# Values from normalised x, tile-wise first FFN blocks behind an interleaved LayerNorm, and doubled tail loads, in a fused LayerNorm, attention and FFN kernel

## Chip, cores and metric

The kernel runs on one core of one Trainium2 chip. Its time is the device time of one execution in microseconds (us). A profile records one execution: its span runs from the first to the last instruction. PE is TensorE, DVE VectorE, ACT ScalarE, POOL GpSimd, and SP the engine that issues most of the DMAs. ACT issues some as well.

## What is computed

One block over x of 2048 tokens by 448, in bf16. All three results are added.

```python
def _layernorm(x, axis=-1, eps=1e-5):
    m = jnp.mean(x, axis=axis, keepdims=True)
    v = jnp.var(x, axis=axis, keepdims=True)
    return (x - m) / jnp.sqrt(v + eps)

# A: attention with feature maps, H = 16 heads of Dh = 28
qkv = (x @ wqkv).reshape(B, S, 3, H, Dh)            # then q, k, v by head
pq, pk = q @ w_phi, k @ w_phi                       # per head
phi_q = concat([softmax(pq), softmax(-pq)]);  phi_k = concat([softmax(pk), softmax(-pk)])
kv = einsum("bhsf,bhsd->bhfd", phi_k, v);     z = phi_k summed over s
o  = (phi_q @ kv) / (phi_q . z + 1e-6);       A = o @ wo
# B: FFN with F = 1792
B = silu(x @ w1) @ w2

x = A_x
xn = _layernorm(x, axis=-1)
return x + _A_ref(xn, A_wqkv, A_w_phi, A_wo) + _B_ref(xn, B_w1, B_w2)
```

## The kernel before

The whole input, all weights and all intermediate values stay on the chip. The 2048 tokens are held as 16 tiles of 128 (`x_sb[:, t]`). Two tiles make a pair `p`, 0 to 7; pairs 0 to 3 are chunk 0, pairs 4 to 7 chunk 1. The 448 columns of x don't divide by 128: they are three blocks of 128 and a tail of 64. Two tiles of a pair share the tail block: the transposed input `xnT` has seven blocks, 0 to 2 (`JA`) for one tile, 4 to 6 (`JB`) for the other, and block 3 (`JT`) with the tail of one tile in partitions 0 to 63 and that of the other in 64 to 127. So the last 64 rows of a weight are needed in both halves of the partitions. Most matmuls run on 64 rows, two at a time in the two halves (`halves`): that is a pair of matmuls. A unit of 7 pairs is given to PE as two halves, `way` 0 (three pairs and the tail pair) and `way` 1 (three pairs).

Stages, in order of time:

1. Start-up, to about 19 us: load x and weights, LayerNorm statistics on DVE (`ln_stats`, L625 and L627), the power -1/2 on POOL (`ln_rstd`, L638), the norm on DVE (`ln_norm`, L647), transposes on PE, their eviction on ACT or DVE (L694, L668), and the first FFN blocks: f-blocks 0 to 7 on pair 0 alone (`ffn1_full`, 128-row matmuls of 128 columns), then 8 to 13 on pairs 0 and 1 (`ffn1_unit` with two f-blocks and 256 columns).
2. To about 33 us the rest of the first FFN layer of chunk 0, and `fold`: products of the projection weights and w_phi, from weights that DVE has transposed (`wq_tr`).
3. To about 66 us keys, values and queries, with exp on ACT (`k_macro`, `v_macro`, `q_group`), the sums `phi_k` on DVE and POOL.
4. The first FFN layer of chunk 1 beside the attention on DVE, and then the second FFN layer, the output projection and the stores.

The order on PE is written out by hand: operations are put in the list `W`, and `weave` makes each of them follow the one before. DVE's order is written out by `chain`. What is left free is ordered by a list scheduler with estimated durations. An engine executes its instructions in that order, so one that waits holds up those behind it. A DMA waits on its own queue only for what it depends on; the loads of the second half of x (`load_x1`, four of them) and of the q and k weights (`load_wqk`) each wait until an earlier load in the list `quarters` has landed (`few`).

In the kernel before, the values of pairs 0 and 1 are made early from x that isn't normalised: `tr_full(p, True, ...)` transposes raw x, `v_raw` multiplies it by the value weights (`Wkv` columns 448 to 896, loaded as `wv`), `col_sums` makes the column sums of these weights, `v_keep` evicts the raw values (ACT), and later `v_scale` (POOL, L724) and `v_fix` (DVE, L731) correct them with the mean and the power, which four small DMAs (`rm_move`, L1078) bring into the order of tokens. The last 64 rows of w1 are loaded into partitions 0 to 63 (two DMAs on the ACT queue) and copied to 64 to 127 by DVE (columns 0 to 511, L1058) and ACT (the other 1280). The last 64 rows of the value weights are loaded twice, once by SP and once by ACT. The loads of the start-up, in program order:

```python
load_x0(0)
load_k(Wkv, D, A_wqkv, 2 * D, 3 * D, "wv", "act")
load_x0(1)
load_tails(Wkv, D, A_wqkv, 2 * D, 3 * D, "wv")
for c0, c1 in ((0, 512), (512, 1024), (1024, 1280), (1280, FF)):
    quarters.append(load_k(w1_sb, c0, B_w1, c0, c1, "w1"))
```

Of the kernel before, what the change touches and what calls it, by code (L numbers as in the profile page):

```python
# [6 lines left out]
BF16 = mybir.dt.bfloat16  # L7
# [346 lines left out]
def bass_parallel_sum__linear_kernel_hedgehog__dense_activation_silu__prompt_kernel(  # L354
# [18 lines left out]
    with es:  # L373
# [37 lines left out]
        halfs = sb("halfs", [128, 128], BF16)  # L411
        hT1 = hT[:, 1].rearrange("p f r i q t -> p (f r i q t)")
        Ek = [Ek4[:, b] for b in range(4)] + [hT1[:, 4096 + 1920 * b:4096 + 1920 * b + EKS] for b in range(4)]
        spare = hT[:, 1].rearrange("p f r i q t -> p (f r i q t)")[:, 2 * FT * 128:]
        xrT = spare[:, 0:2 * 7 * 128].rearrange("p (b j t) -> p b j t", b=2, j=7)
        csum = spare[:, 1792:1792 + 2 * D].bitcast(F32)
        Vraw = spare[:, 2688:2688 + 8 * D].bitcast(F32).rearrange("p (b r c) -> p b r c", b=2, r=2)
# [8 lines left out]
        rm = sb("rm", [128, 2, NT], F32)  # L426
        rmP = sb("rmP", [128, 2, 4], F32)
# [82 lines left out]
        P.op("pool", d_pool(128, 0.5), lambda e: e.memset(halfs[:], 0.5), writes=[halfs[:]], name="halfs")  # L510
# [9 lines left out]
        NWARM = 6  # L520

        def warm(us=220.0):
            w, x = (nc.const_aps.tensor(1.0, [128, n], BF16) for n in (128, 512))
            o = P.op("pe", us, lambda e: e.matmul(banks[7][:], w, x, start=True, stop=True, skip_group_check=True),
                     writes=[banks[7][:]], name="warm")
            o.mode = "full"
            o.pieces = [(us, 2)]
            return o

        for i in range(NWARM):  # L530
            warm(426.0)
# [12 lines left out]
        def load_x0(q):  # L544
            if q > 0:
                load(xt_sb[:, 0, q], xa[0][:, q], 256 * D * 2, f"x0{q}")
                return
            for r, eng in ((0, "sp"), (1, "act")):
                d = slice(D * r, D * r + D)
                load(xt_sb[:, 0, q, d], xa[0][:, q, d], 128 * D * 2, "x00", eng)  # L550
# [8 lines left out]
        def load_tails(dst, d0, src, c0, c1, name):  # L559
            w = c1 - c0  # L560
            return [load(dst[64 * h:64 * h + 64, 3, d0:d0 + w], src[384:448, c0:c1], 64 * w * 2, f"{name}t{h}", ("sp", "act")[h])
                    for h in range(2)]
# [27 lines left out]
        load_x0(0)  # L590
        load_k(Wkv, D, A_wqkv, 2 * D, 3 * D, "wv", "act")
        load_x0(1)
        load_tails(Wkv, D, A_wqkv, 2 * D, 3 * D, "wv")
        for c0, c1 in ((0, 512), (512, 1024), (1024, 1280), (1280, FF)):
            quarters.append(load_k(w1_sb, c0, B_w1, c0, c1, "w1"))
            if c0 == 0:
                for b0, b1 in ((0, 512), (512, FF)):
                    load(w1_sb[0:64, 3, b0:b1], B_w1[384:448, b0:b1], 128 * (b1 - b0), "w1t", "act")
            if c0 in (0, 1024):
                load_x0(2 + c0 // 1024)  # L600
# [33 lines left out]
        def ln_rstd(t0, t1):  # L634
            v2, mm2, r2, nh = ve[:, t0:t1], mv[:, t0:t1, 1], rm[:, 0, at(t0):at(t1 - 1) + 1], neghalf[:, t0:t1]
            o = P.op("dve", 180, lambda e: e.tensor_scalar(v2, mm2, EPS_LN, None, ALU.add),  # L636
                 reads=[mm2], writes=[v2], name="ve")
            P.op("pool", 580, lambda e: e.tensor_tensor(r2, v2, nh, ALU.pow), reads=[v2, nh], writes=[r2], name="rstd")  # L638
            return o

        def ln_norm(p, t, eng="dve"):
            sl, m, r = p % NXN, mv[:, t, 0:1], rm[:, 0, at(t):at(t) + 1]
# [31 lines left out]
        def tr_full(p, raw, bs, engs=("act", "act")):  # L674

            t0, t1 = ln_tiles(p)
            dst = [banks[bs + (j > 2)][:, 128 * (j - 3 * (j > 2)):128 * (j - 3 * (j > 2)) + 128] for j in range(7)]
            if raw:
                xs = [x_sb[:, t, 128 * j:128 * j + 128] for t in (t0, t1) for j in range(3)]
                xs[3:3] = [None]  # L680
            else:
                xs = [xn_sb[:, p % NXN, 128 * j:128 * j + 128] for j in range(7)]
            ops = []
            for a, b in ((0, 3), (3, 7)):
                parts = [(dst[j], xs[j], perm4[:], True, True) for j in range(a, b) if xs[j] is not None]
                ops.append(pe(parts, [62.0] * len(parts), "x_tr" if raw else "xnT_tr", "full"))
            if raw:
                ops.append(pe([(dst[3][64 * r:64 * r + 64], x_sb[:, (t0, t1)[r], 384:448], perm4[:], True, True) for r in range(2)],
                              [62.0], "x_tr", "c64"))
            for (r, j0, j1), eng in zip(((0, 0, 3), (1, 3, 7)), engs):  # L690
                src = banks[bs + r][:, 0:128 * (j1 - j0)].rearrange("p (j t) -> p j t", t=128)
                d = xrT[:, p, j0:j1] if raw else xnT[:, j0:j1, 0, 128 * p:128 * p + 128]
                if eng == "dve":
                    chain([P.op("dve", d_dve(_cols(src)), lambda e, d=d, src=src: e.tensor_copy(d, src), reads=[src], writes=[d],  # L694
                                name="xnT_ev")])
                else:
                    act(d, src, ACTF.Identity, "x_ev" if raw else "xnT_ev")
            return ops

        def v_raw(p):  # L700

            b0 = 2 * p
            main = []
            for r in range(2):
                for k in range(3):
                    main.append((banks[b0 + r][:, 0:D], xrT[:, p, 4 * r + k], Wkv[:, k, D:2 * D], k == 0, False))
            return [pe(main[3 * r:3 * r + 3], [slot(D)] * 3, "v", "full") for r in range(2)], \
                lambda: pe(halves((banks[b0][:, 0:D], xrT[:, p, JT], Wkv[:, 3, D:2 * D]),
                                  (banks[b0 + 1][:, 0:D], xrT[:, p, JT], Wkv[:, 3, D:2 * D]), 0, False, True), [slot(D)], "v")

        def v_keep(p):
            src = psum[:, 1024 * p:1024 * p + 1024].rearrange("p (r c) -> p r c", r=2)[:, :, 0:D]
            act(Vraw[:, p], src, ACTF.Identity, "v_ev")

        def col_sums(ks):

            return pe([(banks[7][:, 0:D], halfs[:] if k == 3 else ones_bf[:], Wkv[:, k, D:2 * D], k == 0, k == 3) for k in ks],
                      [slot(D)] * len(ks), "csum", "full")

        def v_scale(p, after):  # L720

            for r in range(2):
                raw, m = Vraw[:, p, r], rmP[:, 0, 2 * p + r:2 * p + r + 1]
                P.op("pool", 1400, lambda e, raw=raw, m=m: e.tensor_scalar(raw, raw, m, None, ALU.mult),  # L724
                     reads=[raw, m], writes=[raw], name="v_scale").odeps.add(after.id)

        def v_fix(p, after):
            for r in range(2):
                dst, m = vaug[:, p, r, :, 0:DH], rmP[:, 1, 2 * p + r:2 * p + r + 1]
                r3, c3 = (a.rearrange("p (h d) -> p h d", h=H) for a in (Vraw[:, p, r], csum))  # L730
                P.op("dve", d_dve(D), lambda e, dst=dst, r3=r3, c3=c3, m=m: e.scalar_tensor_tensor(  # L731
                    dst, c3, m, r3, ALU.mult, ALU.add), reads=[Vraw[:, p, r], csum, m], writes=[dst], name="v_fix").odeps.add(after.id)
# [67 lines left out]
        def ffn1_unit(c, f0, nf=1, q0=0, nq=4):  # L800
# [8 lines left out]
            for way in range(2):  # L809
                parts = []  # L810
                for i in range(nf):
                    ws = slice((f0 + i) * 128, (f0 + i) * 128 + 128)
                    da, db = (banks[b0 + r][:, n * i:n * i + n] for r in range(2))
                    for k in range(3):
                        parts += halves((da, w1_sb[:, k, ws], xa[JA + k]), (db, w1_sb[:, k, ws], xa[JB + k]),
                                        way, way == 0 and k == 0 and i == 0, way == 1 and k == 2)
                    if way == 0:
                        w = w1_sb[:, 3, ws]
                        parts += halves((da, w, xa[JT]), (db, w, xa[JT]), 0, False, False)
# [13 lines left out]
        def ffn1_full(f0, bs, tails_first):  # L833

            main, tails = [], []
            d2 = [banks[bs + r] for r in range(2)]
            for r, j0 in ((0, JA), (1, JB)):
                for i in range(4):
                    ws, cs = slice((f0 + i) * 128, (f0 + i) * 128 + 128), slice(128 * i, 128 * i + 128)
                    main += [(d2[r][:, cs], w1_sb[:, k, ws], xnT[:, j0 + k, 0, 0:128], not tails_first and k == 0 and i == 0,  # L840
                              tails_first and k == 2) for k in range(3)]
            for i in range(4):
                ws, cs = slice((f0 + i) * 128, (f0 + i) * 128 + 128), slice(128 * i, 128 * i + 128)
                w, x = w1_sb[:, 3, ws], xnT[:, JT, 0, 0:128]
                tails += halves((d2[0][:, cs], w, x), (d2[1][:, cs], w, x), 0, tails_first and i == 0, not tails_first)

            def rows():
                return [pe(main[a:a + 12], [slot(128)] * 12, "ffn1", "full") for a in (0, 12)]

            def rest():  # L850
                return pe(tails, [slot(128)] * 4, "ffn1")
# [5 lines left out]
            return rows, rest, out  # L857
# [39 lines left out]
        def kv_unit(p, c0, name):  # L897
# [566 lines left out]
```

## Time and profile before

| what | value |
|---|---|
| runs | 151.93, 152.47, 154.23 us; median 152.47 |
| profiled execution | 151.9 us, of which the span is 150.2 |
| granted TensorE clock, mean | 1.000 |
| PE busy | 145.3 us, 97% of the span |
| DVE, ACT, POOL busy | 114.9, 86.1, 53.0 us |
| first instruction of PE | 0.82 us |
| last eviction on DVE | 147.29 to 147.91 us |

The profile's page is followed by views of the trace: windows (busy time of each engine in a stretch of the span, with the share of the 16 DMA engines and their rate), the timeline (instructions in order of time, runs of equal ones merged), the DMA issues (KB and the time from issue to landing) and the chain that ended last (followed back from the last instruction). In the names, `big` is the weight w1, `wbig` holds the weights of values, keys and queries, `xu` the normalised x, `x_sb` the input, `hT` the hidden layer and some scratch space, `EqT` scratch space too in the start-up. The matmuls of the working stages all have line L468, since one helper issues them; the first ones, on constants, are L524.

### The profile page before, as it was taken

How to read it: one execution, taken by the hardware profiler on the slowest of the kernel's cores; microseconds unless marked ns; L12 is line 12 of the kernel's file. 1: busy time of each engine (PE TensorE's matmuls, PEld its weight loads, DVE VectorE, ACT ScalarE, POOL GpSimd, SP SyncE). 2: the span in 40 equal slices, each digit the busy share in tenths (PEclk: the TensorE clock that was granted, in tenths of full speed). 3: DMA queues.
4: the chain of work that ended last, by engine and by line, in shares of the span. 5: the costliest groups of instructions: out<-in, count | busy, mean ns of one | idle time of the engine just before them, and what ended most of it. 6: DMA issues, size and time to landing. Idle time of an engine off the chain costs nothing.

```text
span 150.2 us, 5219 instructions
## 1 busy us (share of the span) xinstructions
PE 145.3 (97%) x2328; PEld 84.0 (56%) x2328; DVE 114.9 (77%) x191; ACT 86.1 (57%) x102; POOL 53.0 (35%) x55
## 2 busy tenths in 40 slices
PE   7999999999999999999999999999999999999992
PEld 2578886565545444444555545555555555448771
DVE  0898699997999998575308999999899999940072
ACT  3668868998979788999678998323322200000000
POOL 4322989979609999779300000000000000000000
PEclk9999999999999999999999999999999999999999
DMA  4998761000133543200143444450030003001013
GB/s 140 329 295 160 193 151 34 4 4 4 48 91 91 142 124 98 90 4 0 27 119 86 129 103 137 139 177 22 4 124 0 4 0 127 0 0 65 0 65 122
DMA packets 15588, 12.98 MB, mean 86 GB/s; under 512 B 5838, under 2 KB 14990, under 8 KB 15566
## 3 DMA queue, kind: packets, MB, share of 16 engines
q1 hardware_dynamic: 14782, 11.90, 28.8%
q10 hardware_dynamic: 784, 0.75, 1.6%
q8 instruction: 18, 0.29, 0.8%
q14 instruction: 4, 0.03, 0.1%
HBM read 9.89 MB, written 1.84 MB: 78 GB/s over the span
## 4 chain that ended last, share of the span: by engine, by line
PE 82%; ACT 8%; DMA 4%; issue 2%; ACTq 1%; DVE 0%
PE psum L468 82%; DMA big<-in_B_w_dram 4%; ACT hT L499 3%; ACT EqT L499 3%; ACT L499 1%; ACTq L536 1%; ACT big L499 1%; DVE big L1269 0%; ACTq L1404 0%; ACT tiny L499 0%
## 5 line engine op out<-in xcount | busy, mean ns | idle before, releaser
L468 PE MATMUL psum<-xnT,big 64*128 64x512 bf16 (+4 forms) x540 | 45.8, 313 | 0.6 <-ACT hT L499 0.6
L468 PE MATMUL psum<-w_sb,hT 64*128 64x448 bf16 (+1 forms) x504 | 44.4, 329 | 0.0
L499 ACT ACTIVATE hT<-psum 128x1024 bf16<-128x1024 f32 (+6 forms) x45 | 39.7, 918 | 7.3 <-PE psum L468 7.0
L468 PEld LDWEIGHTS psum<-xnT,big 64*128 64x128 bf16 (+1 forms) x540 | 25.4, 94 | 15.5 <-ACT hT L499 1.3
L468 PEld LDWEIGHTS psum<-w_sb,hT 64*128 64x128 bf16 x504 | 23.6, 94 | 17.3 <-issue 1.3
L499 ACT ACTIVATE big<-psum 128x896 bf16<-128x896 f32 (+1 forms) x16 | 14.8, 955 | 12.3 <-DVE scr L1218 7.2
L468 PE MATMUL psum<-wbig,xnT 64*128 64x448 bf16 x196 | 21.3, 349 | 0.0
L1269 DVE TENSOR_TENSOR big<-psum,x_sb 128x896 bf16<-128x896 f32 (+1 forms) x9 | 8.7, 986 | 12.1 <-PE psum L468 12.1
L499 ACT ACTIVATE EqT<-psum 128x1024 bf16<-128x1024 f32 x16 | 15.6, 1038 | 3.3 <-PE psum L468 3.3
L468 PEld LDWEIGHTS psum<-wbig,xnT 64*128 64x128 bf16 x196 | 9.7, 94 | 9.5 <-ACT big L499 0.3
L468 PE MATMUL psum<-xnT,wbig 64*128 64x512 bf16 x112 | 14.6, 377 | 0.1
L946 POOL TENSOR_TENSOR big<-big,Rk 128x1792 bf16<-128x1792 bf16 x4 | 12.8, 3210 | 5.0 <-DVE Rk L943 4.7
L946 POOL TENSOR_TENSOR hT<-hT,Rk 128x1792 bf16<-128x1792 bf16 (+1 forms) x5 | 12.9, 2606 | 2.1 <-DVE Rk L943 1.1
L625 DVE BATCH_NORM_STATS2 st<-x_sb 128x6 f32<-128x448 bf16 x16 | 9.8, 612 | 4.6 <-DMA x_sb<-in_A_x_dram 3.6
L499 ACT ACTIVATE xu<-psum 128x960 f32<-128x960 f32 x8 | 7.8, 976 | 7.8 <-PE psum L468 4.3
L468 PE MATMUL psum<-wbig,big 32*128 32x448 bf16 (+1 forms) x252 | 11.3, 327 | 0.0
L938 DVE TENSOR_REDUCE Sk<-hT 128x64 f32<-128x1792 bf16 (+1 forms) x5 | 8.2, 1634 | 3.1 <-ACT hT L499 3.1
L638 POOL TENSOR_TENSOR rm<-ve,neghalf 128x2 f32<-128x2 f32 (+1 forms) x9 | 6.2, 691 | 9.9 <-DVE ve L636 9.9
L647 POOL TENSOR_SCALAR xu<-x_sb,mv,rm 128x64 bf16<-128x64 bf16 (+1 forms) x8 | 9.0, 1130 | 0.7 <-POOL rm L638 0.4
L468 PEld LDWEIGHTS psum<-wbig,big 32*128 32x128 bf16 x252 | 6.9, 93 | 4.1 <-issue 1.1
L1224 DVE STREAM_TRANSPOSE big<-big 128x896 bf16<-128x896 bf16 x8 | 8.9, 1110 | 0.2
L1222 DVE TENSOR_TENSOR big<-scr 128x896 bf16<-128x896 f32 x8 | 8.7, 1093 | 0.3
(74 smaller groups left out, 140.4 us busy)
## 6 DMA issues: line engine op xcount, KB each, us to landing
x_sb<-in_A_x_dram SPq DMA_DIRECT2D x4, 448.0 KB, 3.4
x_sb<-in_A_x_dram SPq DMA_DIRECT2D x7, 224.0 KB, 5.6
wbig<-in_A_wo_dram SPq DMA_DIRECT2D x4, 392.0 KB, 3.5
out_dram<-big SPq DMA_DIRECT2D x7, 224.0 KB, 2.0
big<-in_B_w_dram SPq DMA_DIRECT2D x3, 384.0 KB, 7.1
xnT<-hT SPq DMA_DIRECT2D x16, 56.0 KB, 2.0
w_sb<-in_B_w_dram SPq DMA_DIRECT2D x2, 448.0 KB, 3.7
EqT<-in_A_wqkv_dram SPq DMA_DIRECT2D x3, 224.0 KB, 4.0
```

The lines of the kernel that those rows point to most:

```text
L468: r = e.matmul(dst, lhsT, rhs, start=start, stop=stop, skip_group_check=True)
L499: return P.op("act", d_act(_cols(src)), lambda e: e.activation(dst, src, func, scale=scale), reads=[src, *more], writes=[dst], table=table ...
L536: return P.dma(lambda e: e.dma_start(out=dst, in_=src), nbytes, writes=[dst], name=name, eng=eng)
L625: o1 = P.op("dve", 630, lambda e: e.bn_stats(st6[:, t, :], x_sb[:, t, :]), reads=[x_sb[:, t, :]], writes=[st6[:, t, :]], name="bnst")
L638: P.op("pool", 580, lambda e: e.tensor_tensor(r2, v2, nh, ALU.pow), reads=[v2, nh], writes=[r2], name="rstd")
L647: lambda e, xn=xn, xs=xs: e.tensor_scalar(xn, xs, m, r, ALU.subtract, ALU.mult),
L938: P.op("dve", d_dve(896 * n), lambda e, S3=S3, E3=E3: e.tensor_reduce(S3, E3, AXL.X, ALU.add), reads=[E3], writes=[S3], name="Sk")
L946: P.op("pool", d_pool(896 * n, 1.55), lambda e, E3=E3, R3=R3, n=n: e.tensor_tensor(E3, E3, R3[:, :, None].broadcast_to([128, 32 * n, DH]), ...
L1222: P.op("dve", d_dve(896), lambda e: e.tensor_tensor(dst, a0, a1, ALU.add), reads=[a0, a1], writes=[dst], name="oadd")
L1224: P.op("dve", d_dve(896), lambda e: e.transpose(dT, dst), reads=[dst], writes=[oT32[:, n, :, 2 * h:2 * h + 2, :]], name="oT")
L1269: P.op("dve", d_dve((c1 - c0) * ni), lambda e: e.tensor_tensor(dst, src, xs, ALU.add), reads=[src, xs], writes=[dst], name="out_ev")
```

## The change

- The path over raw x goes: `v_raw`, `v_keep`, `col_sums`, `v_scale`, `v_fix`, `scaled_mean`, the raw form of `tr_full` and the four `rm_move` DMAs. The values of pairs 0 and 1 are made by `v_macro` like those of the other pairs, evicted by ACT.
- Each tail is loaded by one DMA into all 128 partitions, from a source pattern that reads its 64 rows twice (`load_tails`). The copies of w1's tail on DVE and ACT go. The w1 tail comes in three loads (columns 0 to 511, 512 to 1023, the rest), the value weights' tail in one.
- The loads are put in another order: w1's first columns before the value weights. The first x tile pair comes in four DMAs, and five loads besides go to the ACT queue.
- The LayerNorm of the first pairs is taken tile by tile on DVE, statistics of the next tile between a tile's power and its norm.
- `ffn1_full` gives out pieces of six matmuls; they are put between the transposes of pairs 0 and 1. `ffn1_unit` and `kv_unit` can do their two halves in the other order (`ways`).
- The 6 warm-up matmuls of 512 columns become 8 of 512 and 8 of 128, and six more of 128 stand between the first transposes and the first FFN matmuls.

```diff
-        NWARM = 6
...
-        for i in range(NWARM):
-            warm(426.0)
+        for n in [512] * 8 + [128] * 8:
+            warm(n / 1.2, n)
...
+        def load_x0(q, eng="sp"):
+            load(xt_sb[:, 0, q], xa[0][:, q], 256 * D * 2, f"x0{q}", eng)
+
+        def load_x00():
+            for r in range(2):
                 d = slice(D * r, D * r + D)
-                load(xt_sb[:, 0, q, d], xa[0][:, q, d], 128 * D * 2, "x00", eng)
+                for h, eng in ((0, "sp"), (1, "act")):
+                    p = slice(64 * h, 64 * h + 64)
+                    load(xt_sb[p, 0, 0, d], xa[0][p, 0, d], 64 * D * 2, "x00", eng)
...
-        def load_tails(dst, d0, src, c0, c1, name):
-            w = c1 - c0
-            return [load(dst[64 * h:64 * h + 64, 3, d0:d0 + w], src[384:448, c0:c1], 64 * w * 2, f"{name}t{h}", ("sp", "act")[h])
-                    for h in range(2)]
+        def load_tails(dst, d0, src, c0, c1, name, eng="sp"):
+
+            a = src[384:448, c0:c1]
+            return load(dst[:, 3, d0:d0 + c1 - c0], type(a)(a.tensor, a.offset, [[0, 2], *a.ap]), 256 * (c1 - c0), name + "t", eng)
...
-        load_x0(0)
-        load_k(Wkv, D, A_wqkv, 2 * D, 3 * D, "wv", "act")
-        load_x0(1)
-        load_tails(Wkv, D, A_wqkv, 2 * D, 3 * D, "wv")
-        for c0, c1 in ((0, 512), (512, 1024), (1024, 1280), (1280, FF)):
-            quarters.append(load_k(w1_sb, c0, B_w1, c0, c1, "w1"))
-            if c0 == 0:
-                for b0, b1 in ((0, 512), (512, FF)):
-                    load(w1_sb[0:64, 3, b0:b1], B_w1[384:448, b0:b1], 128 * (b1 - b0), "w1t", "act")
-            if c0 in (0, 1024):
-                load_x0(2 + c0 // 1024)
+        load_x00()
+        quarters.append(load_k(w1_sb, 0, B_w1, 0, 512, "w1"))
+        load_x0(1, "act")
+        load_tails(w1_sb, 0, B_w1, 0, 512, "w1")
+        quarters.append(load_k(w1_sb, 512, B_w1, 512, 1024, "w1", "act"))
+        load_tails(w1_sb, 512, B_w1, 512, 1024, "w1")
+        load_x0(2, "act")
+        load_k(Wkv, D, A_wqkv, 2 * D, 3 * D, "wv")
+        load_tails(Wkv, D, A_wqkv, 2 * D, 3 * D, "wv", "act")
+        quarters.append(load_k(w1_sb, 1024, B_w1, 1024, 1280, "w1"))
+        load_tails(w1_sb, 1024, B_w1, 1024, FF, "w1")
+        load_x0(3, "act")
+        quarters.append(load_k(w1_sb, 1280, B_w1, 1280, FF, "w1"))
...
-        x_tr = [tr_full(p, True, 2 * p) for p in range(2)]
-        t0, t1 = ln_tiles(0)
-        chain([*ln_stats(t0), ln_rstd(t0, t1), *ln_stats(t1), ln_rstd(t1, t1 + 1)])
-        ln_norms(0)
-        scaled_mean(0)
...
+        (a0, a1), (b0, b1) = rows(0)
+        chain([*ln_stats(a0), ln_rstd(a0, a1), *ln_stats(b0)])
+        chain(ln_norm(0, a0))
+        chain([ln_rstd(b0, b1)])
+        first, rest = ln_stats(ln_tiles(1)[0])
+        chain([first])
+        chain(ln_norm(0, b0))
+        chain([rest])
+        (a0, a1), (b0, b1) = rows(1)
+        chain([ln_rstd(a0, a1), *ln_stats(b0)])
+        chain(ln_norm(1, a0))
+        chain([ln_rstd(b0, b1)])
+        ln_first(2)
+        chain(ln_norm(1, b0))
+        chain(ln_stats(ln_tiles(2)[1]))
+        tr0 = tr_full(0, BK_T)
+        f0, f0_rest, f0_out = ffn1_full(0, 6)
+        f4, f4_rest, f4_out = ffn1_full(4, 0)
+        tr1 = tr_full(1, BK_T, ("act", "dve"))
+        chain([ln_rstd(ln_tiles(2)[0], ln_tiles(2)[1] + 1)])
+        W.append((tr0[0], *[warm(60.0, 128) for _ in range(6)], f0[0], tr0[1], f0[1], *f4[:2], *f0[2:], *f4[2:], tr1[0]))
+        r0, r4 = f0_rest(), f4_rest()
...
+        v0 = v_macro(0, "act", (1, 0))
+        u = ffn1_unit(0, 8, 2, 0, 2, (1, 0))
...
+        w = ffn1_unit(0, 10, 2, 0, 2)
+        tr2 = ln_tr64(2, ("act", "dve"))
+        W.append((r0, tr1[1], v0[0], r4, v0[1], u[0], w[0], u[1], tr2))
+        late_consts()
+        u = ffn1_unit(0, 12, 2, 0, 2)
...
+        tr3 = ln_tr64(3, ("act", "dve"))
         ln_first(4)
...
+        v1 = v_macro(1, "act")
+        W.append((u[0], w[1], v1[0], tr3, u[1], v1[1]))
...
-        v_scale(0, norms(5))
+        norms(5)
...
-        v_scale(1, norms(7))
+        norms(7)
...
-        v_fix(0, dprev[-1])
```

## Prediction

> **What bounds the kernel now.** I read the page's first two parts, then the chain that ended last, then the start-up in the timeline, then the DMA views, since the change touches only the first 20 us and some work that hung on it.
>
> From the page, the busy times and the slices:
>
> ```profile
> PE 145.3 (97%) x2328; PEld 84.0 (56%) x2328; DVE 114.9 (77%) x191; ACT 86.1 (57%) x102; POOL 53.0 (35%) x55
> DMA  4998761000133543200143444450030003001013
> ```
>
> From the chain that ended last, in order of time (start, us, what):
>
> ```profile
> 3.22 6.46 DMA big<-in_B_w_dram
> ...
> 9.71 1.27 ACT big L499
> ...
> 11.00 0.93 ACT hT L499
> ...
> 11.97 13.70 PE psum L468 x256
> 25.67 0.13 issue
> 25.80 34.06 PE psum L468 x472
> ...
> 71.29 75.97 PE psum L468 x1208
> ```
>
> PE sets the end: from 11.97 us on it hardly stands. Of the 4.9 us it is idle, 0.8 lie before its first instruction and 2.9 behind its last. So a delay of PE in the start-up comes out at the end nearly whole, and a gain is bounded by the time at which the dense stretch begins. Up to 11.97 us the chain is a load of the last 64 rows of w1 (160 KB, landed at 9.7 us), its copy to the other half on ACT, and one keep of raw values. The slices show the DMA engines full from 2 to 14 us.
>
> The windows of the start-up (columns: length, busy time of PE, PEld, DVE, ACT, POOL, granted clock, DMA share, GB/s) give the rate of one DMA engine:
>
> ```profile
> 4.00:5.00 1.00, 1.00 (x13) 0.58 (x11) 0.90 (x5) 0.91 (x2) 0.51 (x1) 1.00 1.10 351
> 6.00:7.00 1.00, 1.00 (x7) 0.49 (x5) 0.89 (x3) 0.05 (x1) 0.27 (x2) 1.00 1.04 353
> 7.00:9.00 2.00, 2.00 (x17) 1.07 (x14) 1.69 (x7) 1.52 (x3) 0.54 (x1) 1.00 1.08 238
> ```
>
> With the share at 1.0, 353 GB/s over 16 engines is 22 GB/s each; the trace's packets agree (1024 B in 46 ns, 896 B in 41 ns, undisturbed).
>
> The DMA issues of the first 9 us (KB, then us from issue to landing), and PE's timeline:
>
> ```profile
> big<-in_B_w_dram SPq DMA_DIRECT2D x3, 384.0 KB, 7.1
> big<-in_B_w_dram ACTq DMA_DIRECT2D x1, 160.0 KB, 6.5
> wbig<-in_A_wqkv_dram SPq DMA_DIRECT2D x1, 56.0 KB, 4.0
> phi<-in_A_w_phi_dram SPq DMA_DIRECT2D x1, 24.5 KB
> ```
>
> ```profile
> 9.73 1.51 PE L468 MATMUL psum<-xnT,big 128*128 128x128 bf16 x24
> 11.97 2.72 PE L468 MATMUL psum<-xnT,big 128*128 128x128 bf16 x48 [0.33 <-ACT hT L499]
> 14.73 2.57 PE L468 MATMUL psum<-xnT,big 64*128 64x256 bf16 x44
> 17.33 2.89 PE L468 MATMUL psum<-xnT,big 64*128 64x256 bf16 x50
> ```
>
> The phi line is the one to notice: alone in the list it has no time to landing. Each DMA engine that takes part in a load ends its share with a 4-byte packet. The 5 issues of the ACT queue left 80 of these (16 each). The 60 issues of the SP queue left 958, two short of 960: one load ran on 14 engines. Phi is the load whose outermost count, 28, does not divide by 16 but by 14; its 448 pieces in all would have divided by 16. So a load is dealt out in equal parts along its outermost dimension.
>
> **The change, part by part.** I name the w1 column loads q0 (0 to 512), q1 (512 to 1024), q2 (1024 to 1280), q3 (the rest), and the tails t0, t1, t2 (64 last rows of w1) and wvt (of wv).
>
> *The tails.* Each is now one load whose source is a pattern with an outermost count of 2 and stride 0, then 64 rows. By the phi row it is dealt to 2 engines, one copy each. No load of before has an outermost count under 28, so this is the unknown price. One end: all 16 engines share it, and it costs only its bytes, 560 KB at about 340 GB/s, 1.7 us of full DMA against 336 KB before. Other end: two engines carry it alone. I take the second, the phi row being nearest. The Trainium skill, "DMA: Bandwidth & Descriptors", section "Why a DMA increments its semaphore by 16 and not by 1", says the same of both sides of a load: the engine count is the largest number up to 16 that divides the slowest dimension of source and destination. By that rule too the tails run on 2 engines.
>
> Bytes on such an engine (1/16 of each normal load, 64 whole rows of each tail), in KB. SP queue, in order: x00 7, q0 25, t0 66, t1 66, wv 22, q2 12, t2 98, q3 25: 320. ACT queue: x00 7, x01 14, q1 25, x02 14, wvt 57, x03 14: 132. Together 452 KB at 22 GB/s are 20.5 us, and the first packets run at 2.1 us. If the queues share the engine equally while both hold work, ACT's is empty at 14.1 us, and the loads are complete at: q0 5.0, q1 6.3, x02 7.6, t0 10.9, wvt 12.8, x03 14.1, t1 15.5, wv 16.5, q2 17.0, t2 21.5, q3 22.6 (today q3 is issued at 5.5 and takes 9.1: 14.6). The other 14 engines are done by about 10 us, and that doesn't help.
>
> *PE in the start-up.* Removed: 16 raw transposes (1.66 us), 4 column sums and 12 raw-value matmuls, all before 9 us. Added: values of pairs 0 and 1 by tiles, 14 pairs of 448 columns (34 such matmuls took 3.44 us at 37.5 us, so 0.20 a pair): 2.8 us less 0.4 of tails done today. The first normalised tile is ready at about 5.5 us (x at 3.3, then statistics 0.63+0.18+0.15, power 0.58 on POOL, with the second tile's statistics inside it, norm 0.39), transposes 0.2, eviction 0.5: first FFN matmuls at 6.6, where today they come at 9.0. The order on PE is written out. f0, f4 and the transposes (24 full matmuls 1.3 to 1.5, twice, plus 0.5) keep PE busy to about 10.3; f0's tail waits for t0, 10.9; second transposes to 11.4. Then v0 needs wv: PE stands to 16.5, and behind it in its queue stand u8, f10, f12, which have their x. v0 (7 pairs 1.4), f4's tail (0.25) and half of u8 (6 pairs of 256 columns at 0.117, from 44 in 2.57 us: 0.7) end at 18.9. Next is f10, whose columns are in q3 and t2: PE stands to 22.7. From there to the end of this group: 36 pairs of 256 columns 4.2, v1 1.4, two transposes of 0.37: 6.3, end 29.0.
>
> Today the same group (without values) ends at 17.33 + 24/50 of 2.89 = 18.7. **Loss 10.3 us.**
>
> *What runs beside it.* x1's third part is issued only when q3 has landed; today its last part lands 4.1 us behind q3, so 26.8 instead of 18.7. VectorE goes on with statistics behind its eviction of the third transposes, at about 28.5 instead of 18.86: 9.6 later. Its transposes for the first fold end at 35.3 and PE is there at 36.0, so this is hidden by 0.7. xn_move leaves 10 us later and its first user too.
>
> *Off the path.* w1copy (ACT 1.27, DVE 0.29), raw evictions and csum on ACT (4.3), four v_fix on DVE (about 0.65 each, 37.8 to 44), four v_scale on POOL (1.4 each), mur and four rm_move (1 KB): nothing, because PE is dense in 33 to 66 us (32.90 of 33.00 us). At most the 0.1 of idle comes back there, so I take 0.1. The two new value evictions on ACT (0.95 each) lie beside PE's standing. ACT has two DMA issues more (0.4 to 0.9 each), before its first eviction at 5.9.
>
> Sum: 10.3 - 0.1 = 10.2. The profiled execution spans 150.2 and took 151.9, 1.7 around it; it becomes 160.4 and 162.1. The median of the runs, 152.47, is 0.57 higher: 162.7. The few edits that I priced at nothing can only take, and the undisturbed packets leave some air: **162.4 us**. Its own range: at 25 GB/s an engine (1792 B in 72 ns, the fastest packets) q3 lands at 20.2, 160; with 2 us at the 238 GB/s of 7 to 9 us and the clock below, 166. Another order of the two queues moves q3 little, the last load of all, but can hide 2 us more: 158.
>
> **Rivals.**
> 1. *The clock.* In 0.82 to 3.54 us six matmuls of 512 columns took 2.72, 0.45 each, twice 0.21, though the granted clock reads 1.00. PE starts slow, and after standing 5.1 and 3.8 us may start slow again. Nothing before stands over 0.5 us, so the price lies between 0 and what the first 4.4 us lost, 2.2: 164.6. A slow start behind the first stand costs nothing, since the 2.4 us of work there stretch into the second stand; only one behind the second counts, 3.8 us or what is then left of it. The Trainium skill, "TensorE: Matmul & The Clock Gate", part 1, has PE fall to half clock behind an idle window of some 3.4 us, and by it the second stand decides.
> 2. *Not slower: the tails go to 16 engines*, dealt by the destination's 128 partitions (phi has 28 on both sides and can't tell). Then 3.2 MB at the rate of today bring q3 between 12.5 and 14.6 us, PE wants it at 13. Its work from 6.6 on is 12.4 (f0 and f4 2.8, transposes 1.4, tails 0.5, values 2.8, 42 pairs of 256 columns 4.9) and ends at 19.0, or 20.6 with the wait for q3; VectorE's chain (14.3 of work from 3.3, about 1.1 of waits) lets the next unit start at 18.7. Against 18.7 today that is 152.8 to 154.4, take 153.0. It decides from the point where q3 lands before 15 us.
> 3. *Faster by over 3 us*: would need dense PE from 9 us and the added 2.4 us free. PE's idle inside the span is 1.2 us; almost excluded.
>
> **How the numbers follow.** Forecast 0.70, the clock 0.17, 16 engines 0.11, faster 0.02. Slower by over 2% (about what a measurement of this kernel can tell from no change, 3 us) is 0.87, within 0.11, faster 0.02. The range 158 to 166 holds the first two but for their tails, some 8 in 10; 153.0 is left outside.
>
> **What would show it.** Right: q3's issue-to-landing near 17 us instead of 9.1, t2 about as late; DMA share falling to about 0.12 (2 of 16) between 10 and 22 us; PE idle some 5 us for wbig and some 4 for big; PE dense again from about 23 us; nothing else different behind 35 us. Wrong: every issue of the start landed by 15 us, with the share near 1 up to then.

## The result, and the profile after

| kernel | median (lowest to highest) | beside it, the kernel before | ratio, 95% interval |
|---|---|---|---|
| after | 165.72 us (164.76 to 166.97, 4 runs) | 152.2 us (4 runs) | 1.0906 [1.0801, 1.1011] |

The change makes the kernel 9% slower, 13.5 us by the medians. The profiled execution is the longest of the four: 166.97 us with a span of 165.0, 14.8 more than the span before. Runs of a kernel that lie over 1.5% above its fastest are left out of every ratio here, and where such a run was the profiled one (e7), its trace is not read.

The lines of the page that answer to those shown of before (busy times, the granted clock and the DMA share in 40 slices of 4.1 us):

```profile
PE 150.2 (91%) x2336; PEld 87.8 (53%) x2336; DVE 112.5 (68%) x188; ACT 82.4 (50%) x95; POOL 47.2 (29%) x49
PEclk9879695799999999999999999999999999999998
DMA  3951735800000335243002434343303001101013
```

PE's busy time grew by only 4.9 us, so some 10 of the 14.8 are standing (PE waits). The DMA share falls to a tenth in the fourth slice (12 to 16 us) and to three tenths in the sixth (21 to 25 us), and the clock is down in five of the slices two to eight. Before, the share stayed at eight tenths or more from 3.8 to 15 us.

The chain that ended last (start, us, what):

```profile
4.26 4.77 SPq L527
...
9.08 1.84 SPq L527
...
10.96 12.54 DMA big<-in_B_w_dram
23.49 1.61 issue
25.10 49.61 PE psum L462 x698
...
86.15 75.91 PE psum L462 x1208
```

The first part is new: SP itself stands for 4.77 us over the issue of one load (wv), then for 1.84 over the next (q2). Then a load issued at 10.96 is awaited; that is t2, which landed at 23.5. PE is dense from 25.10 us, not from 11.97. The last part, 75.91 us, is as long as before (75.97): behind the start-up nothing changed. The 1.61 us of "issue" ahead of 25.10 have a cause that the chain doesn't name. It is q3, whose issue on SP comes behind t2's, as the timeline of SP shows (start, us), and its line in the DMA issues of 12 to 20 us:

```profile
12.81 3.42 SPq L527 DMA_DIRECT2D big<-in_B_w_dram  x1
```

```profile
big<-in_B_w_dram SPq DMA_DIRECT2D x1, 384.0 KB, 12.2
```

Issued from 12.81 on, with 3.42 us for the issue alone, q3 landed 12.2 us later, at 25.0. A later load of SP, x1's third part, which waits for q3, is issued at 25.03.

The DMA issues of the first 9 us (KB, then us from issue to landing):

```profile
wbig<-in_A_wqkv_dram SPq DMA_DIRECT2D x1, 336.0 KB, 13.7
big<-in_B_w_dram SPq DMA_DIRECT2D x2, 128.0 KB
wbig<-in_A_wqkv_dram ACTq DMA_DIRECT2D x1, 112.0 KB
```

The new tails (t0 and t1 of 128 KB, wvt of 112) have no time to landing, which before was so for phi alone. wv needs 13.7 us; the same load takes 6.4 in e1 below, where only the tails are loaded differently.

PE's timeline (start, us, line, operation, tiles, shape, count, and what it waited for):

```profile
7.45 0.82 PE L462 MATMUL psum<-xnT,big 128*128 128x128 bf16 x6 [0.56 <-DMA big<-in_B_w_dram]
...
13.04 0.40 PE L462 MATMUL psum<-xnT,big 64*128 64x128 bf16 x8 [0.90 <-DMA big<-in_B_w_dram]
...
17.98 1.30 PE L462 MATMUL psum<-wbig,xnT 64*128 64x448 bf16 x6 [4.21 <-DMA wbig<-in_A_wqkv_dram]
...
25.10 3.59 PE L462 MATMUL psum<-xnT,big 64*128 64x256 bf16 x32 [3.40 <-issue]
```

And the windows of the two stands (the stretches in which PE waits) and of what follows each (length, busy time of PE, PEld, DVE, ACT, POOL, granted clock, DMA share, GB/s):

```profile
14.00:16.00 2.00, 0.00 (x0) 0.00 (x0) 0.88 (x3) 0.50 (x1) 0.70 (x1) 1.00 0.14 49
...
18.00:20.00 2.00, 2.00 (x18) 1.12 (x20) 1.13 (x5) 0.25 (x1) 1.50 (x5) 0.50 0.74 200
...
22.00:24.00 2.00, 0.00 (x0) 0.00 (x0) 0.00 (x0) 0.00 (x1) 1.88 (x2) 1.00 0.14 46
...
26.00:28.00 2.00, 2.00 (x22) 1.61 (x20) 0.00 (x0) 0.00 (x0) 0.00 (x0) 0.50 0.66 154
```

While PE stands for wv (4.21 us) and for q3 (3.40), the share is 0.14: 0.14 of 16 engines is 2.2 engines. Behind each stand the granted clock is 0.50: the 32 matmuls of 256 columns at 25.10 take 3.59 us, 1.92 at full clock in e1. The group of f-blocks ends at 33.6 us against 18.7 before: 14.9 us lost, and the span grew by 14.8.

### The profile page after: what moved, and what is told of

Same layout as the page of the kernel before. It is cut to its first block, busy times and chain, and to the rows that moved or that the text cites. A ratio compares the mean times of both kernels' runs of the same rounds, so it can differ in the third digit from the quotient of the medians.

```text
span 165.0 us, 5216 instructions
## 1 busy us (share of the span) xinstructions
PE 150.2 (91%) x2336; PEld 87.8 (53%) x2336; DVE 112.5 (68%) x188; ACT 82.4 (50%) x95; POOL 47.2 (29%) x49
## 3 DMA queue, kind: packets, MB, share of 16 engines
HBM read 10.12 MB, written 1.84 MB: 72 GB/s over the span
## 4 chain that ended last, share of the span: by engine, by line
PE 76%; DMA 8%; SPq 6%; ACT 6%; issue 3%; DVE 0%; ACTq 0%
PE psum L462 76%; DMA big<-in_B_w_dram 8%; SPq L527 6%; ACT EqT L493 3%; ACT hT L493 2%; DVE big L1208 0%; ACTq L1343 0%; ACT tiny L493 0%; ACT L493 0%
## 5 line engine op out<-in xcount | busy, mean ns | idle before, releaser
L462 PE MATMUL psum<-xnT,big 64*128 64x512 bf16 (+4 forms) x540 | 50.7, 332 | 5.1 <-issue 3.4
L493 ACT ACTIVATE hT<-psum 128x1024 bf16<-128x1024 f32 (+2 forms) x38 | 35.5, 964 | 18.8 <-PE psum L462 18.6
L462 PEld LDWEIGHTS psum<-xnT,big 64*128 64x128 bf16 (+1 forms) x540 | 29.3, 102 | 20.9 <-issue 4.7
L462 PE MATMUL psum<-wbig,xnT 64*128 64x448 bf16 x224 | 25.7, 362 | 4.2 <-DMA wbig<-in_A_wqkv_dram 4.2
L493 ACT ACTIVATE big<-psum 128x896 bf16<-128x896 f32 (+1 forms) x18 | 16.6, 949 | 12.4 <-DVE scr L1157 7.3
L462 PEld LDWEIGHTS psum<-wbig,xnT 64*128 64x128 bf16 x224 | 11.1, 96 | 15.1 <-DMA wbig<-in_A_wqkv_dram 4.4
```

The costliest lines, as they stand in the source:

```text
L462: r = e.matmul(dst, lhsT, rhs, start=start, stop=stop, skip_group_check=True)
L493: return P.op("act", d_act(_cols(src)), lambda e: e.activation(dst, src, func, scale=scale), reads=[src, *more], writes=[dst], table=table ...
```

## The experiments

In the diffs, lines without a sign are those of the kernel named.

**e1, two loads for each tail.** The kernel after, each tail as two loads of 64 rows, one to each half of the partitions, on the same queue.

```diff
-            return load(dst[:, 3, d0:d0 + c1 - c0], type(a)(a.tensor, a.offset, [[0, 2], *a.ap]), 256 * (c1 - c0), name + "t", eng)
+            return [load(dst[64 * h:64 * h + 64, 3, d0:d0 + c1 - c0], a, 128 * (c1 - c0), name + "t", eng) for h in range(2)]
```

> The changed kernel with each tail loaded by two DMAs of 64 rows, one for each half of the partitions, in place of one DMA whose source pattern counts 2 outermost. All else is as changed: order of loads, values from normalised x, LayerNorm order, order on TensorE. Theory (the tails ran on two DMA engines and everything behind them on these engines came late): the tails go to 16 engines, the last columns of w1 land by 13 to 15 us instead of 25, TensorE's stands of 4.2 and 3.4 us go, 152 to 155 us. Rival (the new order costs by itself: values of pairs 0 and 1 in the start-up, behind the normalisation, with all of TensorE's queue behind them): at most 3 us of the 13 come back, 162 or more.

Measured: 154.4 us (153.9 to 155.16, 4 runs), before 151.97; ratio 1.0157 [1.0086, 1.0228]. Of the 13.5 us lost, about 11 come back, with the same bytes to the same places. The waits of PE that are left in e1's timeline:

```profile
15.49 1.92 PE L462 MATMUL psum<-xnT,big 64*128 64x256 bf16 x32 [1.19 <-DMA big<-in_B_w_dram]
...
21.75 7.04 PE L462 MATMUL psum<-xnT,big 64*128 64x256 bf16 x112 [0.42 <-DVE xnT L663]
```

q3 has landed at 15.3 us instead of 25.0, and the clock never leaves 1.00. So what the pattern does to the spread over the engines is the cause of most of the loss. The second line points at the third transposes' eviction on VectorE. All engines of e1 in order of time around it:

```profile
17.98 1.24 POOL L985 MEMSET big<- 128x256 bf16 x1
18.32 2.64 DVE L1032 COPY phi<-phi 28x448 bf16<-28x448 bf16 x3
...
19.28 1.24 POOL L986 MEMSET big<- 128x768 bf16 x1
```

The three small copies of phi take 2.64 us (1.04, 1.27, 0.27) where an undisturbed one takes 0.27; the first two end 0.13 us behind the end of a memset on POOL each (19.22 and 20.52).

**e2, the doubled pattern in the kernel before.** All tails by the new pattern (`load_tails` as in the kernel after), those of w1 on ACT's queue as before and that of the value weights on SP's alone; the two copies of w1's tail removed, nothing else.

```diff
...
-                    load(w1_sb[0:64, 3, b0:b1], B_w1[384:448, b0:b1], 128 * (b1 - b0), "w1t", "act")
+                    load_tails(w1_sb, b0, B_w1, b0, b1, "w1", "act")
...
-        chain([P.op("dve", d_dve(512, 2), lambda e: e.tensor_copy(wd[0], ws[0]), ...
-        act(wd[1], ws[1], ACTF.Identity, "w1copy").odeps.add(xe.id)
```

> The kernel before with one part of the change alone: its tails of w1 (columns 0 to 511, and the other 1280) and of the value weights each come by one DMA with the doubled source pattern, and the copies of w1's tail to the other half go. Values from raw x, order of loads and order on TensorE stay as before. Theory of the two engines: 451 KB on each of them at 22 GB/s, the long tail complete at about 22 us, and the matmuls of f-block 8, which want it at 13.3, wait: 160 to 164 us. Rival (order): 152 to 153, as before.

Measured: 161.99 us (161.72 to 162.42, 4 runs); ratio 1.0655 [1.0591, 1.0718]. The pattern alone costs the old kernel 10 us. PE's first long wait is here:

```profile
14.39 0.53 PE L468 MATMUL psum<-wbig,ones_bf 128*128 128x448 bf16 x1 [7.82 <-DMA wbig<-in_A_wqkv_dram]
```

It stands 7.82 us for the value weights, of which only the tail is loaded in the new way; the raw path needs them first. After that the chain runs over the third tile pair of x, which landed at 19.5 us after 16.3 on its way, and its LayerNorm on VectorE; PE is dense from 27.2. So every load that shares the two engines is late, not only the tails and w1. The size is that of the two-engine theory; the place of the wait was not foreseen.

**e3, only wv's tail by two loads.**

```diff
+            if name == "wv":
+                return [load(dst[64 * h:64 * h + 64, 3, d0:d0 + c1 - c0], a, 128 * (c1 - c0), name + "t", eng) for h in range(2)]
```

> The changed kernel with the value weights' tail alone by two DMAs of 64 rows; the three tails of w1 keep the doubled pattern. Theory of the two engines, by bytes: 57 KB less on each engine become 7, so the last columns of w1 land 2.3 us earlier, and the time falls by about 2.3 us, to 163. Theory that only the wait for the value weights counts, not the bytes on the engines: no change below 165, since these weights themselves are loaded as before.

Measured: 164.0 us (162.85 to 164.32, 4 runs); ratio 1.077 [1.0694, 1.0846], 1.7 under after. The stand for wv shrinks from 4.21 to 2.75 us, and q3's matmuls begin at 23.42 instead of 25.10. Each of the two engines has 50 KB less to carry (57, less the 7 that are its sixteenths of the new loads), 2.2 us at 23 KB a us; 1.7 came. So the tails add up along these two engines, and one tail of 112 KB is worth that much.

**e4, constant matmuls in the stands.** The kernel after, with 16 matmuls on constants ahead of the first value unit and 12 ahead of f-block 10. They compute nothing that is used.

```diff
-        W.append((r0, tr1[1], v0[0], r4, v0[1], u[0], w[0], u[1], tr2))
+        W.append((r0, tr1[1], *fill1, v0[0], r4, v0[1], u[0], *fill2, w[0], u[1], tr2))
```

> The changed kernel with TensorE kept at work on constants in its two stands: 16 matmuls of 512 columns before the first value unit and 12 before f-blocks 10 and 11 (banks 3 and 5, results not used). They are to end before the loads that TensorE waits for. Theory of the clock (behind the stands TensorE runs at half its clock, which cost 2.2 us from 25 to 33 us): granted clock 1.0 from 25 us on and 2 to 2.5 us faster, 163. If the granted clock of 0.5 costs nothing here because loads set the pace anyway: no change, 165.

Measured: 163.1 us (162.85 to 163.54, 4 runs); ratio 1.0719 [1.0645, 1.0794], 2.6 under after with more work on PE. From its timeline and windows:

```profile
24.69 1.92 PE L462 MATMUL psum<-xnT,big 64*128 64x256 bf16 x32 [0.65 <-issue]
```

```profile
26.00:30.00 4.00, 4.00 (x92) 3.62 (x89) 2.09 (x6) 2.96 (x5) 0.00 (x0) 1.00 0.83 213
```

q3's matmuls begin nearly when they did (24.69 against 25.10), but the clock behind is 1.00, and the group takes 5.7 us (24.69 to 30.35) instead of 8.5 (25.10 to 33.6). So the low clock behind a stand is worth 2.6 to 2.8 us here, and it is PE's idling that brings it.

**e5, the loads without the copies in the kernel before.** w1's tail by 64-row loads to both halves, the copies removed.

```diff
+            if c0 in (0, 512):
+                b0, b1 = (0, 512) if c0 == 0 else (512, FF)
+                load(w1_sb[64:128, 3, b0:b1], B_w1[384:448, b0:b1], 128 * (b1 - b0), "w1t")
```

> The kernel before, with w1's tail loaded to both halves of the partitions by loads of 64 rows (the second halves on the SP queue, behind the columns 0 to 511 and 512 to 1023) and without the copies on DVE and ACT: the aim of one part of the change, by loads that 16 engines share. Values from raw x as before. Theory: ACT's copy of 1.27 us (9.71 to 10.97) and the keep behind it come forward, and TensorE's idle of 0.33 and its wait before f-block 4 go; but the fold's transposes on DVE hold TensorE at 25.8 us, so 0 to 0.5 us faster, 151.5 to 152. Rival (224 KB more to load, 0.7 us of full DMA, make x's third part and the last columns of w1 late): 0.5 to 1 us slower.

Measured: 153.34 us (152.54 to 154.88, 12 runs), before 152.04 (17 runs); ratio 1.0082 [1.0041, 1.0122]. Slightly slower, by less than 2%. The chain that ended last shows a part of why:

```profile
11.24 5.03 DMA x_sb<-in_A_x_dram
16.29 3.88 DMA EqT<-in_A_wqkv_dram
20.19 3.15 DMA EqT<-in_A_wqkv_dram
...
26.10 34.05 PE psum L468 x472
```

PE reaches f-block 4 earlier (11.36 us instead of 11.97), but the 224 KB more push x1 and the key and query weights back, VectorE's transposes of these end later, and the fold starts at 26.10 instead of 25.80. That is 0.3 us, in the trace of a run of 152.54; where the rest of the 1.3 us between the medians lies isn't shown. So replacing these copies by loads is no gain here even with a good spread.

**e6, phi's copies later.** e1, with phi's copies behind the third transposes' eviction, out of the memsets' way.

```diff
+        tr3 = ln_tr64(3, ("act", "dve"))
         for g in range(1, 4):
             dst = phi32[32 * g:32 * g + DH]
...
-        tr3 = ln_tr64(3, ("act", "dve"))
```

> The changed kernel with two loads for each tail, and DVE's three copies of phi behind the eviction of the third transposes instead of ahead of it. With the copies ahead, they took 2.64 us in all beside two memsets on POOL (1.2 in the kernel before), and TensorE waited 0.42 for that eviction. Theory (the residue over before is made of small waits, of which this is one): 0.4 to 0.6 faster than with the copies ahead (154.4), 153.9. If the fold's transposes on DVE set TensorE's time behind it, the copies only move: no change.

Measured: 154.38 us (153.68 to 158.09, 6 runs), before 152.04; ratio 1.0116 [1.0054, 1.0177]. In the trace the edit does what it should: the copies take 0.87 in all, PE no longer waits for the eviction, the group ends at 20.62 instead of 21.3 and the fold starts at 27.76 instead of 28.72; the profiled span falls from 153.3 to 152.3. Over the runs a difference to e1 is not resolved (1.0116 and 1.0157, their intervals overlap).

**e7, q3 ahead of t2.** e6, with q3 issued before t2 and f-block 10's tail part taken last.

```diff
-        load_tails(w1_sb, 1024, B_w1, 1024, FF, "w1")
         load_x0(3, "act")
         quarters.append(load_k(w1_sb, 1280, B_w1, 1280, FF, "w1"))
+        load_tails(w1_sb, 1024, B_w1, 1024, FF, "w1")
...
-        w = ffn1_unit(0, 10, 2, 0, 2)
+        w = ffn1_unit(0, 10, 2, 0, 2, (1, 0))
```

> As the one before, and the last columns of w1 loaded ahead of their tail, f-blocks 10 and 11 with their tails in the second half. With the tail ahead, TensorE stood 1.19 us for these columns. Theory (residue of small waits): the columns land 0.6 us earlier and the wait halves, 153.2 to 153.5. Rival (the residue is the work added, 2.4 us of value matmuls that now stand in TensorE's dense stretch, whatever waits): no change against the one before.

Measured: 154.25 us (153.09 to 157.31, 6 runs); ratio 1.0117 [1.0052, 1.0182]. No difference to e6 is resolved: the gain that the theory promised, 1 us at most, is no larger than what these intervals leave open (0.6% to either side), and whether q3 landed sooner isn't shown.

**e8, less value work.** e6, with 8 of the 14 pairs of value matmuls of token pairs 0 and 1 left out, so that these values are incomplete.

```diff
+            K = 1 if name == "v" and p < 2 else 3
...
-                for k in range(3):
+                for k in range(K):
```

> The kernel after with each tail as two 64-row loads and the phi copies later (e6: span 152.3, dense stretch from 14.96, group end at 20.62, fold at 27.76), and of the value matmuls of pairs 0 and 1 only the first of three column blocks and the tail (3 of 7 pairs each; the values of these two pairs are incomplete). 8 pairs go, 0.19 each, 1.5 us: 0.75 before the wait for q3, 0.75 behind it. Theory (the residue over the kernel before is the value work that moved from the idle start-up into the dense stretch): the half behind the wait comes out whole, and of the half before it what the wait for q3 (0.67 now) does not take up; group end 19.1 to 19.9, span 150.8 to 151.6, time 152.3 to 153.5. Rival (loads and VectorE bind, not PE's work): the wait for q3 grows by the first half, and the fold still waits for VectorE's transposes of the q and k weights, which end at 27.66 in e6: fold not before 27.3, span 152 or more, time 154.

Measured: 153.75 us (153.13 to 155.13, 6 runs), before 152.11; ratio 1.0128 [1.0082, 1.0175]. My theory fell. The wait for q3 and the start of the fold in its timeline:

```profile
15.15 1.92 PE L462 MATMUL psum<-xnT,big 64*128 64x256 bf16 x32 [1.69 <-DMA big<-in_B_w_dram]
...
27.57 0.65 PE L462 MATMUL psum<-phi,scr 32*128 32x28 bf16 x64
```

With 1.5 us of work gone, the wait for q3 grows from 0.67 to 1.69 us and the fold moves by 0.19 us, to where VectorE's transposes for it end (25.00 + 2.48 = 27.48). The value matmuls are not the residue: loads and VectorE end nearly as late as PE.

**e9, pair 1's values while q3 is awaited.** e6, with the value unit of pair 1 put ahead of f-block 10; nothing is left out.

```diff
-        W.append((r0, tr1[1], v0[0], r4, v0[1], u[0], w[0], u[1], tr2))
+        W.append((r0, tr1[1], v0[0], r4, v0[1], u[0], *v1, w[0], u[1], tr2))
...
-        W.append((u[0], w[1], v1[0], tr3, u[1], v1[1]))
+        W.append((u[0], w[1], tr3, u[1]))
```

> The whole of e6 (each tail as two 64-row loads, phi copies later; span 152.3, time 154.4) with the value unit of pair 1 put ahead of f-block 10 in PE's order: its operands are there from 12 us, while f-block 10 waits for q3. Theory (PE has run out of other work when it waits for q3; the residue is that wait plus the added value work): the wait of 0.67 goes, the value unit takes its place, f-block 10 starts at 15.6 to 15.8, group end 20.0, fold at 27.2, span 151.7, time 153.7. Rival (VectorE is late next: in e8, with less work on PE, its transposes for the fold ended at 27.48 and the fold stood for them): the third transposes come no earlier, VectorE's chain from their eviction to the fold takes 8.0 again, and the fold stays at 27.6 or later: span 152.2, time 154.2. Neither gets below the kernel before, since PE has 12.4 of work behind its first FFN matmul at 7.0.

Measured: 156.31 us (155.87 to 157.34, 6 runs), before 152.28; ratio 1.0261 [1.0206, 1.0315]. Worse, and by neither theory. PE's new waits:

```profile
20.14 1.70 PE L462 MATMUL psum<-xnT,big 64*128 64x256 bf16 x28 [0.92 <-ACT hT L493]
...
24.32 7.03 PE L462 MATMUL psum<-xnT,big 64*128 64x256 bf16 x112 [1.61 <-DVE st L620]
```

The wait for q3 does go, as the theory had it. But ScalarE has one more eviction ahead of the hidden layer's, and PE stands 0.92 us for it. The second wait is named for VectorE, whose operation had nothing to do with it; ScalarE's half of the third transposes' eviction ended at 24.26 (23.71 + 0.55), behind 1.94 us of two activations. The two waits are 2.5 us. (This profiled run was also 1 us late at its first FFN matmul, 7.99 instead of 7.02; the other five runs have spans of 154.4 to 155.6, still 2 us or more above the 152.3 of e6's profiled run. Whether the same two waits make up their loss isn't shown.)

## Why the prediction was right, and where its sizes were off

Forecast 162.4 us in 158 to 166, slower with 0.87; measured 165.72, 3.3 above and just inside. Point by point:

- *PE sets the end, and only the start-up matters*: right. Group end +14.9, span +14.8, nothing different behind it. The off-path removals are worth nothing that shows: PE is busy in every one of the 31 us from 35 to 66.
- *The tails run on two engines*: right, by the share of 0.14 (2.2 engines), the missing landing times, and e1, where the same bytes over all engines bring back 11 us. The closing packets settle it: by the prediction's count, a load shared by all 16 engines leaves 16 packets of 4 bytes. In the trace of after the 56 issues of SP left 852 of them, 44 short of 896 (14 each for t0, t1 and t2, 2 for phi), and the 7 issues of ACT left 98, 14 short of 112 (wvt): two engines for each tail. In e1 only phi's 2 are missing. Where nothing but the two engines is at work (13 to 16 us and 22 to 24), they move 45 to 49 GB/s together, some 23 to 24 each; 22 was taken. The Trainium skill, "DMA: Bandwidth & Descriptors", section "Why a DMA increments its semaphore by 16 and not by 1", has the engine count as the largest number up to 16 that divides both sides' slowest dimension; the share measured here agrees.
- *Two stands of PE, for wv and for q3*: right in place and nearly in size: forecast 5.1 and 3.8, measured 4.21 and 3.40. But everything is later than the sum had it: first FFN matmuls 7.45 instead of 6.6 (q0 landed at 7.4, not 5.0, since in 2 to 4 us the engines moved only 130 GB/s; the second part of the first x tile pair also held VectorE up by 0.72, but q0 came last), f0's tail 13.04 instead of 10.9, wv 18.0 instead of 16.5, q3 25.0 instead of 22.7. **The first mis-sized term is that of q3: 2.4 us.** The trace shows three things that the working left out. In 2 to 4 us the 130 GB/s are 8 an engine instead of 22, which puts each engine some 1.3 us behind. In 20 to 22 us the packets of t2 (1536 B) took 134 to 142 ns instead of 65, beside the loads of x1: 34 packets, some 1.2 us on each of the two engines. Both are estimates from the packets, and a rate of 23 instead of 22 gives about 0.9 back, so how the 2.4 us divide stays open. Third, SP could not issue the loads at once: wv, q2, t2 and q3 took 4.77, 1.84, 1.81 and 3.42 us, so that q3's issue began at 12.81 and the other 14 engines stood empty instead of being served early. That this delayed q3 isn't shown: nothing shows the two engines that it waited for without work (the share is 0.13 or more in each microsecond from 4 to 25).
- *q3's issue to landing near 17 us*: it reads 12.2, because the issue itself, which I had at about 5.5, began at 12.81. The landing is late as forecast; the sign that I named for it was wrong, since it took the issues for free. The share fell to some 0.14 as named, but only in 13 to 16 and 22 to 26 us: in between, the loads that SP issued late ran on the other engines.
- *The group behind, 6.3 us*: it took 8.5. **The second mis-sized term, 2.2 us, is the low clock of rival 1**, added to the forecast rather than in its place. e4 shows it as a cause: with the stands filled, the group took 5.7 us. That the 2.2 is rival 1's upper bound to the tenth is luck: the low clock cost 2.8 (8.5 against 5.7), and the 6.3 of the sum was 0.6 too much for a group at full clock. The Trainium skill, "TensorE: Matmul & The Clock Gate", part 1, puts half clock behind an idle window of some 3.4 us; the first stand agrees (PE idle from 13.94 to 17.35 us, clock 0.50 from there), but ahead of the second fall, at 24.18 us, PE had still worked 0.94 of the 3.41 us, so a wholly idle window wasn't needed here. The forecast kept it out of the sum because no stand of before was longer than 0.5 us; after the long stands of this kernel it belonged into it.
- *The two terms together*: 4.6 us, the whole excess of the profiled span (165.0 against 160.4). The profiled run is 1.25 us above the median of the runs, so the time is only 3.3 above the forecast.
- *The first slow stretch is free*: right. Behind the first stand 18 to 21 us ran at half clock and went into the wait for q3.
- *The fold hidden by 0.7*: hidden by 1.0 (transposes end at 39.6, PE is there at 40.65).
- *Rival 2* didn't happen, but e1 and e6 are its kernel. It put the end of the group at 19.0, or 20.6 with the wait for q3, and took 153.0; e6 has 20.62 and 154.4, its upper bound. Even with the tails well spread the change doesn't gain.

What stays open is the last 1 to 2% of e1 and e6. PE begins its FFN 2 us sooner than before and ends the group 1.9 later, with the value work (2.6 us) and the waits for wv and q3 (0.83 and 0.67 in e6) in between. e8 and e9 each eased one of these, and each time another was late: q3 and VectorE in e8, ScalarE in e9. I can't name one of them as the bound. No version run is below the kernel before.

## What to carry to other kernels

Before a load is written with a repeated or a short outermost dimension, count how many engines that dimension can be dealt to, and add up what each of them then carries from all loads in flight; the late ones are the innocent loads on the same engines. Price a stand of several us twice: its length, and the slower clock of the work behind it (2.8 us here). And when a load or a unit is moved to fill a wait, look which engine evicts its result: in e9 that cost more than the wait.

## What the runs showed of the hardware that I had not expected

- An issuing queue stands still behind a backlog on few engines: SP needed 11.8 us for four issues (wv, q2, t2, q3), each of which takes 0.5 to 0.6 in e1, and for a part of that time 14 of 16 engines were idle (share 0.14 in 13 to 16 us, 0.29 to 0.37 in 8 to 10).
- The granted clock fell to 0.50 without a long stand, too. In the profiled run of after PE was idle for 1.62 us (4.6 to 6.2) and 0.56, and the clock was at 0.50 from about 7.1 to 10.5; in e9 waits of 0.93 and 1.56 did the same (0.50 in 8 to 11 us); in e6 0.78 and 0.44 did not. Thus it seems to go by how much PE did over some microseconds, not by a single gap. The traces say how much: their records of the clock change only in steps of 3.41 us, and in all traces but that of e7, while the clock was at 1.00, it fell to 0.50 behind each step in which PE was busy for 1.57 us or less (eight steps; 1.57 is after, 3.70 to 7.11) and behind none in which PE was busy for 1.72 or more (1.72 is e8, 12.72 to 16.13). At 0.50, 2.49 us busy (after, 24.18 to 27.59) did not bring it back and 2.78 (after, 17.35 to 20.76) did. This is read from the traces; no run was made to test it.
- A copy on VectorE stood for a memset on POOL: 1.04 and 1.27 us instead of 0.27, each until 0.13 us behind the memset's end. The Trainium skill, "SBUF — State Buffer", section "SBUF: two separate sides", calls the port pair of the two an exclusive lock held for a whole instruction; e1 agrees, and in e6, away from the memsets, the three copies took 0.87.
